# Tokens dealt to partitions four in a row: 4 KB runs of DRAM per partition in place of four 1 KB runs

## The chip, the cores and the metric

The kernel runs on one core of one Trainium2 chip. The metric is the device time of one execution in microseconds (us); each kernel was run several times. Ratios are the mean time of one kernel's fast runs over the mean time of the other's fast runs of the same rounds, with a 95% interval, so they are not quite the ratio of the medians that stand beside them.

Names: TensorE (PE in the profile) multiplies matrices, VectorE (DVE) and ScalarE (ACT) work elementwise, SyncE (SP) issues DMAs. A "tile" is 128 tokens, one on each partition; a "chunk" is four tiles, 512 tokens.

## The reference, cut to what matters

```python
x = A_x                                   # 2048 tokens x 512, bf16
x = x + A(layernorm(x), wqkv, wo)         # linear attention, 32 heads of 16
x = x + B(layernorm(x), w1, w2)           # 512 -> 1376, relu, -> 512
x = x + A(layernorm(x), wqkv, wo)
x = x + B(layernorm(x), w1, w2)

# inside A: every token's k and v are summed over all tokens, no mask
kv  = einsum("bhsd,bhse->bhde", phi(k), v)
z   = einsum("bhsd->bhd", phi(k))
o   = (phi(q) @ kv) / (phi(q) . z)
```

Everything but `kv` and `z` is done token by token, and those two are sums over all tokens. So it doesn't matter which token sits on which partition, as long as the output is written back through the same assignment.

## The kernel before

The program builds a list of 1316 operations, and two tables then fix the order of the instructions on every engine (`ORDER`) and the PSUM bank, the buffer that a matmul writes to, of every result (`BANKS`). Each engine gets its instructions in that order.

```python
# token n*128 + p sits in tile n on partition p
x_v   = A_x[0].rearrange("(n p) d -> p n d", p=128)
out_v = out[0].rearrange("(n p) d -> p n d", p=128)
def ld_x(t, lo=0):                                       # one chunk, 512 KB
    dma(lambda e, t=t: e.dma_start(xin[:, 4*t+lo:4*t+4, :], x_v[:, 4*t+lo:4*t+4, :]), ...)
dma(lambda e: e.dma_start(xin[:, 0, :], x_v[:, 0, :]), ...)   # tile 0 alone, 128 KB
ld_x(0, 1)                                               # tiles 1 to 3, 384 KB
dma(... wqkv[:, :, D:2*D] ...)                           # key weights, 512 KB
for t in range(1, NCH):
    ld_x(t)
    if t == 1: dma(... wqkv[:, :, 0:D] ...)              # query weights
# [cut: value weights, wo; w1 and w2 much later]

# TensorE starts with ten dummy matmuls; nothing else is ready yet
for k in range(WARM): last = e.matmul(psv[:, wt, :], wrm[:, 0:128], wrm[:, :], ...)

# chunk 0: per tile, statistics (VectorE), 1/std (ScalarE), norm (VectorE),
# transposes (TensorE), copy to Tb (ScalarE or VectorE), key projection (TensorE)

def store_chunk(t):          # chunks 0 to 2: one DMA; the last chunk: tile by tile
    for (lo, hi) in segs:
        dma(lambda e, lo=lo, hi=hi: e.dma_start(out_v[:, lo:hi, :], xn[:, lo:hi, :]), ...)
# [cut: everything between]
```

Of the kernel before, what the change touches and what calls it, by code (L numbers as in the profile page):

```python
# [69 lines left out]
class _Graph:  # L70
# [46 lines left out]
    def add_flex(self, alts, reads=(), writes=(), name=""):  # L117
# [7 lines left out]
17 0 14 12 15 18 13 1 16 19 2 20 22 3 24 4 21 23 25 5 6 26 27 7 28 8 47 29 33 30 31 32a 48 34 40 49 35 71 50 36 41 42  # L125
51 37 43 52 72 44 38 73 53d 45 56 87 46a 58 39a 81 89 54 88 60 76 83 59 57 55 61 82 93 62 74 63 78 75 115 98 77 94 79
117 103 95 64 80 65a 108 113 66a 119 86 68a 120 118 116 69 114 92 121 84 67a 122 85 90 135 99 91 70 105 123 141 125d
100 124d 154 104 128 230 109 126d 130 127d 110 156 129 136 132 155 160 131 142 133 138 134 137 158 148 143 101 96 147
150 161 157 159 162 97 144 163 171 139 149 140 145 189 172 146 102 164 177 190 166d 165d 168a 167d 153 169 151 178 152
176 106 191 111 170 107 173 192 183 222 179 112 174 182 9 180 184 193 10 185 223 175 195 11 181 186 188 187 196 219  # L130
220 197 221 213 198 199 207 215 214 201 216 208 217 209 194 203 210 202 200 211 204 205 206 231 212 232 233 218 234
224 261 228 262 225 229 263 226 239 235a 236d 237a 238d 244 240 264 241 259 265 246 242 245 243 266 254 268 260 249
256 270 255 313 269 317 314a 276 267 251 257 315 318a 311 252 271 316a 312d 250 258 339 247 273 248 272 253 334 340
278 277 319 335 329 320 341 336 342d 338 344 330 337a 331 286 332d 333 345 349 321 296 346 288 347d 281 298 322 350
297 323 291 343 299 289 274 287 324 275 306 292 327 293 290 301 307 279 280 308 358 328 303 326 302 370 325 359a 362
371a 309 227 282 388 283 363d 348 398 389 284 392 393 285 399 378 304 403 379 305 394 402 360 404 397 376 294 380 300
405 351 407 310 374 381 361a 382 368 377a 295 375a 390 400 395 383 352 369a 410 437 386 355 438 411 385 396a 364 356d
439 384 372 357 365a 387 406a 366 440 373a 441 457 367a 353 412 354 401a 442 458 447 391a 473 413 409 452 448 462 408
453 451 443 456 480 444 477 461 474 478 493 475 494 445 496 449 450d 417 446 419 476 418a 463 427 420a 454 466 455d
414 479 467 428a 423 459 464 415a 465d 460a 469 425 470 416 471 481 472 424a 495 421 426d 468 497 435 422a 429 572  # L140
436a 433 430a 431 434a 482 432a 484 483 498 488 499 485 489 504 486 500 505 487 501 521 502 503 490 526 491 522 492
506 547 507 525 536 508 509 510 527 531 548a 511 530 512 570 550 513 549 532 552 551a 514 571 515a 554 516d 518a 556
573 519 517a 537 558 553a 520 555a 538 533 560 534d 557a 539d 559a 566 523 528 542 524d 561a 529d 562 567a 543 541 535
564 563d 540 574 565a 544 545 575 546 577 576 568 578 579 569a 581 580 714 590 591 715 582 592 593 583 595 594 584 585
596 597 586 716 618 717 587 598 620 619 588 601 621 629 589 622 602 623 631 599 630 643 632 600 633 625 635 624 626
603 648 645 604 644 606 653 605 607 627 646 650 628 663 608 649 636 664d 655 609 647 654 665 610 670 651 638 652 656
637 666 634 671d 668 667a 611 612a 613d 672 669d 614a 616 674 673d 615a 639 676 675d 617 640 718 677a 657 641 719 678
720 680 679a 723 681a 682 724 721 683a 729 722 684 730 725 685a 734 792 735 793 737 726 736 738 739 794 741 740 731
742 727 745 732 728 796 746 733 743 797 658 798 744 795 801 660 747 659 799 802 748 807 800 812 749 750 751 808 686
752 753 661 754 813 662 687 803 688 814 755 817 756a 757d 809 693 818 758a 810 760 823 695 689 690 815 811 696 691 804  # L150
816 694 759a 642 805 824 806 819 761 697 820 698 825 692 821 826 822 699 827 828 829 700 830 831 706 832 702 701 707
703 833 834d 835a 713 704 709 836d 838 762 708 705 837a 768 764 710 839 769 711 763 765 712 775 771 770 776 766 772
767 783 777 778 782 785 773 779 784 774 873 840 874 780 875 786 781 791 842 841 846 787 843 852 788 848 847 858 854
849 844 853 845 789 860 855 859 851 850 790 857 863 861 856 862 866 876 867 877 864 868 895 865 896 878 897 872d 870a
869d 883 871a 898 879 899 893 880 885 881 900 894 884 888 903 905 890 904 889 902 949 951 950a 925 901 952a 891 945
907 892 947 910 946a 948d 906 908 968 886 911 882 909 912 963 887 927 969 926 973 964 972 913 953 974 967 978 965 954
970 975 966d 930 971d 976a 979 983 955 915 980 932 981d 920 956 917 984 957 916 935 922 914 918 921 958 919 936 940
923 924 937 959 931 1012 962 998 1013 960 942 989 961 1014 992 990a 943 1015 941 991 1006 1016 999a 993d 982 996 933
1007a 928 934 994 997a 929 944 977 1032 938 995a 939 985 1037 1033 1034 1027 1038 1035a 1039 1022 1028 1040a 1029 1008
1031 1023 1043 1030a 1024 1000 1025d 1026 986 1042 987 1004 988 1001d 1041 1044 1109 1010 1005a 1009a 1071 1011a 1017  # L160
1002 1018 1036 1019 1072 1057 1021 1003a 1048 1073 1020 1058a 1051 1107 1049a 1074 1111 1052a 1050 1075 1112 1108 1076
1081 1110 1053 1078 1077 1086 1054a 1079 1055 1080 1087 1059 1056a 1045 1090 1046 1061 1082 1047 1060a 1083 1063 1084d
1062a 1088 1113 1085 1067 1089a 1065 1064a 1101 1068a 1069 1066a 1091 1070a 1096 1092 1093 1095 1114 1097 1125 1094d
1100 1189 1116 1126 1115 1128 1098 1117 1099a 1127 1118 1190 1102 1121 1129 1130 1122 1119 1131 1191 1123 1135 1132
1136 1120 1133 1124 1177 1134 1137 1145 1178a 1138 1192 1139 1140 1146 1150 1141 1149 1155 1151 1144 1147 1166 1142
1156 1148a 1169 1152 1167a 1157 1143d 1154 1153d 1160 1175 1158d 1170a 1103 1104 1159 1171 1105 1162 1106 1161 1176a
1173 1172d 1163 1168 1181 1164 1174a 1165 1179 1182a 1193 1180a 1183 1194 1184a 1185 1195 1196 1186a 1198 1197 1187
1199 1200 1188a 1210 1245 1201 1211 1207 1246 1208 1247 1203 1214 1204 1209 1215 1202 1229 1205 1212 1230a 1206 1225
1213 1216 1222 1226a 1248 1227 1223a 1224 1217 1228a 1233 1218 1219 1231 1234a 1220 1221 1235 1232a 1237 1236a 1239
1238a 1249 1240a 1250 1252 1251 1241 1253 1254 1242a 1243 1255 1259 1244a 1263 1260 1278 1261 1264 1262 1256 1265 1266  # L170
1279 1268 1282 1269 1267 1273 1280 1257 1274 1270 1258 1299 1281 1283 1300 1296 1284 1297 1287 1298 1275 1271 1288
1276 1301 1272 1285 1302 1292 1277 1286 1303 1293 1307 1304 1305 1289 1308 1306 1309 1294 1290 1295 1315 1310 1291
1314 1311 1313 1312
"""
BANKS = ("0145346702076132532532355225315253131235215113532321551212533251266701701076152313542613074562174032"
         "6357657130422400110424124141114204120144220014202421014221040214120410204224101021404031605473414160"
         "275136027534461275403172566403241570613247")
# [46 lines left out]
def build_kernel(nc, A_x, A_wqkv, A_wo, B_w1, B_w2, out, n_layers_pairs=2, Q_LATE=3, O_PE_CHUNKS=3, PHI_PATH=3,  # L224
# [17 lines left out]
    with es:  # L242
# [110 lines left out]

        x_v = A_x[0].rearrange("(n p) d -> p n d", p=128)
        out_v = out[0].rearrange("(n p) d -> p n d", p=128)
        def ld_x(t, lo=0):
            dma(lambda e, t=t: e.dma_start(xin[:, 4 * t + lo:4 * t + 4, :], x_v[:, 4 * t + lo:4 * t + 4, :]),
                [], [("xin", i) for i in range(4 * t + lo, 4 * t + 4)], (1150.0, 2400.0, 1500.0, 1500.0)[t], "ld_x%d" % t)
        dma(lambda e: e.dma_start(xin[:, 0, :], x_v[:, 0, :]), [], [("xin", 0)], 50.0, "ld_x0a")  # L359
        wq_v = A_wqkv.rearrange("(c p) n -> p c n", p=128)  # L360
        ld_x(0, 1)
        dma(lambda e: e.dma_start(wqkv[:, :, D:2 * D], wq_v[:, :, D:2 * D]), [], [("wk",)], 1650.0, "ld_wk", eng=ACT if WK_ACT else SP)
        for t in range(1, NCH):
            ld_x(t)
            if t == 1:
# [445 lines left out]
        def store_chunk(t):  # L811
# [3 lines left out]
            for (lo, hi) in segs:  # L815
                dma(lambda e, lo=lo, hi=hi: e.dma_start(out_v[:, lo:hi, :], xn[:, lo:hi, :]),
                    [("xn", i) for i in range(lo, hi)] + [("T", i) for i in range(NT)], [("out", t, lo)],
                    400.0 * (hi - lo), "st%d_%d" % (t, lo))
# [265 lines left out]
```

## Time and profile before

280.0 us, median of 3 runs (279.91 to 280.34). These lines are from the page of before: busy time of the engines, the chain of work that ended last by engine, and the DMA queue (packets, MB, share of 16 engines' time).

```profile
span 278.0 us, 4780 instructions
PE 273.4 (98%) x1804; PEld 154.2 (55%) x1804; DVE 221.0 (80%) x567; ACT 176.6 (64%) x367; POOL 34.5 (12%) x43
...
q1 hardware_dynamic: 44368, 17.96, 27.8%
...
q14 instruction: 8, 0.07, 0.1%
...
PE 96%; DVE 1%; DMA 1%; ACT 0%; issue 0%; SPq 0%; DVEq 0%
```

TensorE is busy 98% of the span and makes up 96% of the chain; DMA is 1% of it. "Busy" hides small waits: matmuls overlap in the trace (one of 512 columns is listed with 379 ns, and the next can start 216 ns after it). The distances between their starts show the waits. They are 216 ns for 512 columns, 109 ns for 256 and 43 ns for 96. Summed for all 1804 matmuls at those rates this is 267.8 us, and the real distances are only 5.8 us longer.

Where the 1% of DMA lies is seen in the chain in order of time (start, us, what):

```profile
1.25 3.18 DMA xin<-in_A_x_dram
4.43 0.02 issue
4.46 0.69 DVE bst L418
5.15 0.33 DVE xn L845
5.47 0.05 issue
5.52 0.41 PE ps L474 x4
```

The chain waits for tiles 1 to 3 (issued at 1.25 us, landed at 4.43), goes through VectorE and reaches TensorE at 5.5 us. From 6.6 us on it stays on TensorE until 272.8 us. The same stretch in the timeline (start, us, engine, line, operation, in brackets the idle time before and what ended it):

```profile
3.07 0.69 DVE L418 BATCH_NORM_STATS2 bst<-xin 128x6 f32<-128x512 bf16 x1 [1.89 <-DMA xin<-in_A_x_dram]
4.46 0.69 DVE L418 BATCH_NORM_STATS2 bst<-xin 128x6 f32<-128x512 bf16 x1 [0.47 <-DMA xin<-in_A_x_dram]
5.07 0.40 DVE L845 TENSOR_SCALAR xn<-xin,mv,rstd 128x512 bf16<-128x512 bf16 x1
5.52 0.40 PE L474 MATMUL ps<-ident,xn 128*128 128x128 bf16 x4
5.95 0.60 ACT L481 ACTIVATE Tb<-ps 128x512 bf16<-128x512 bf16 x1 [1.41 <-PE ps L474]
6.61 1.04 PE L511 MATMUL ps<-wqkv,Tb 128*128 128x512 bf16 x4 [0.26 <-ACT Tb L481]
```

VectorE waits twice for x (for tile 0, then for tiles 1 to 3), tile 0's norm stands behind the statistics of a later tile, and the first projection (6.61 us) comes 2.17 us after tiles 1 to 3 landed. The part on DMA issues gives the size and the time from issue to landing of each load:

```profile
xin<-in_A_x_dram SPq DMA_DIRECT2D x3, 512.0 KB, 8.1
out_dram<-xn SPq DMA_DIRECT2D x3, 512.0 KB, 2.9
...
xin<-in_A_x_dram SPq DMA_DIRECT2D x1, 384.0 KB, 3.2
...
xin<-in_A_x_dram SPq DMA_DIRECT2D x1, 128.0 KB, 2.3
```

### The profile page before, as it was taken

What the parts mean: (1) busy time and instruction counts of PE and PEld (TensorE: products, weight loads), DVE (VectorE), ACT (ScalarE), POOL (GpSimd) and SP (SyncE); (2) the same over time, 40 slices, a digit from 0 to 9 for tenths busy, and PEclk for the clock granted to TensorE, in tenths of its full rate; (3) what the DMA queues carried; (4) which work ended last, traced back from release to release, by engine and by line L of the source; (5) the groups of instructions that cost most, each with busy time, mean ns of one, the idle gap of its engine ahead of it and who ended that gap; (6) DMA issues with size and microseconds to landing.
All of it is one profiled execution on the core that took longest, in us unless ns stands there. A gap on an engine that the chain in (4) does not pass through costs nothing.

```text
span 278.0 us, 4780 instructions
## 1 busy us (share of the span) xinstructions
PE 273.4 (98%) x1804; PEld 154.2 (55%) x1804; DVE 221.0 (80%) x567; ACT 176.6 (64%) x367; POOL 34.5 (12%) x43
## 2 busy tenths in 40 slices
PE   7999999999999999999999999999999999999995
PEld 2444454444475747755777444544454675675784
DVE  5999759999995796986798786799989497282686
ACT  3998728998856494496157874899894617415100
POOL 3111000000301021042003473000011002000000
PEclk9999999999999999999999999999999999999999
DMA  6976940120314036014004210004131115103004
GB/s 215 348 165 67 297 150 0 24 54 0 59 38 94 2 64 107 2 19 76 2 0 58 57 38 2 0 1 79 22 72 21 38 38 143 29 2 96 0 2 151
DMA packets 44534, 18.32 MB, mean 66 GB/s; under 512 B 36352, under 2 KB 44000, under 8 KB 44512
## 3 DMA queue, kind: packets, MB, share of 16 engines
q1 hardware_dynamic: 44368, 17.96, 27.8%
q8 instruction: 14, 0.23, 0.4%
q10 hardware_dynamic: 144, 0.07, 0.1%
q14 instruction: 8, 0.07, 0.1%
HBM read 7.01 MB, written 2.10 MB: 33 GB/s over the span
## 4 chain that ended last, share of the span: by engine, by line
PE 96%; DVE 1%; DMA 1%; ACT 0%; issue 0%; SPq 0%; DVEq 0%
PE ps L511 95%; DMA xin<-in_A_x_dram 1%; DVE xn L551 1%; PE ps L474 0%; DVE bst L418 0%; ACT Tb L481 0%; DVE xn L805 0%; SPq L359 0%; DVEq L1022 0%; DVE xn L845 0%
## 5 line engine op out<-in xcount | busy, mean ns | idle before, releaser
L511 PE MATMUL ps<-Tb,w 128*128 128x512 bf16 x320 | 73.9, 379 | 0.0
L710 ACT ACTIVATE big<-ps 128x512 bf16<-128x512 f32 x70 | 40.5, 597 | 37.9 <-PE ps L511 37.8
L511 PEld LDWEIGHTS ps<-Tb,w 128*128 128x128 bf16 x320 | 30.8, 98 | 33.2 <-DMA Tb<-xn 0.2
L771 DVE SCALAR_TENSOR_TENSOR xres<-ps,rstdf,xres 128x256 f32<-128x256 f32 x64 | 29.9, 480 | 21.8 <-PE ps L511 21.0
L518 ACT ACTIVATE sqscr<-xres 128x512 bf16<-128x512 f32 x48 | 30.2, 631 | 19.4 <-DVE xres L555 14.9
L493 ACT ACTIVATE escr<-ps 128x512 bf16<-128x512 f32 x64 | 37.8, 614 | 6.2 <-PE ps L511 6.1
L491 ACT ACTIVATE big<-ps 128x512 bf16<-128x512 f32 x64 | 38.4, 617 | 3.8 <-PE ps L511 3.8
L511 PE MATMUL ps<-w,big 128*128 128x256 bf16 (+1 forms) x224 | 34.3, 273 | 0.0
L511 PE MATMUL ps<-wqkv,Tb 128*128 128x512 bf16 x128 | 30.9, 379 | 0.4 <-ACT Tb L481 0.3
L511 PE MATMUL ps<-big,xn 128*128 128x512 bf16 x128 | 31.1, 379 | 0.0
L497 DVE TENSOR_TENSOR big<-big,emscr 128x512 bf16<-128x512 bf16 x64 | 29.3, 469 | 2.2 <-ACT big L491 0.8
L511 PE MATMUL ps<-Tb,wqkv 128*128 128x512 bf16 x128 | 30.4, 379 | 0.0
L511 PE MATMUL ps<-Wp,big 128*128 128x512 bf16 x128 | 30.2, 379 | 0.0
L544 POOL TENSOR_TENSOR rstdf<-varf,nhalf 128x4 f32<-128x4 f32 x8 | 8.9, 1115 | 128.3 <-DVE varf L542 109.2
L511 PEld LDWEIGHTS ps<-w,big 128*128 128x128 bf16 (+1 forms) x224 | 21.7, 98 | 4.9 <-DVE xres L771 0.6
L495 DVE TENSOR_SCALAR emscr<-escr 128x512 bf16<-128x512 bf16 x64 | 19.9, 320 | 4.8 <-ACT escr L493 4.7
L511 PE MATMUL ps<-w2s,xin 128*128 128x256 bf16 x160 | 22.1, 273 | 0.0
L511 PE MATMUL ps<-w,xin 128*128 128x256 bf16 x160 | 22.1, 272 | 0.0
L669 DVE TENSOR_TENSOR big<-big,ps 128x512 bf16<-128x512 bf16 x32 | 20.3, 680 | 1.0 <-PE ps L511 0.8
L511 PEld LDWEIGHTS ps<-Tb,wqkv 128*128 128x128 bf16 x128 | 12.2, 98 | 14.5 <-issue 0.7
L511 PEld LDWEIGHTS ps<-wqkv,Tb 128*128 128x128 bf16 x128 | 12.0, 98 | 14.8 <-ACT Tb L481 1.0
L511 PEld LDWEIGHTS ps<-Wp,big 128*128 128x128 bf16 x128 | 11.9, 98 | 14.9 <-ACT Wp L600 1.0
(103 smaller groups left out, 330.3 us busy)
## 6 DMA issues: line engine op xcount, KB each, us to landing
wqkv<-in_A_wqkv_dram SPq DMA_DIRECT2D x3, 512.0 KB, 7.2
xin<-in_A_x_dram SPq DMA_DIRECT2D x3, 512.0 KB, 8.1
out_dram<-xn SPq DMA_DIRECT2D x3, 512.0 KB, 2.9
w<-in_B_w_dram SPq DMA_DIRECT2D x1, 1376.0 KB, 6.6
w<-in_B_w_dram SPq DMA_DIRECT2D x1, 1280.0 KB, 9.7
wo<-in_A_wo_dram SPq DMA_DIRECT2D x1, 512.0 KB, 9.0
Tb<-xn SPq DMA_TRANSPOSE x30, 3.2
xin<-in_A_x_dram SPq DMA_DIRECT2D x1, 384.0 KB, 3.2
```

What stands on the lines that cost most here:

```text
L491: g.add(ACT, lambda e: e.activation(dst_ap, psv[:, b, :], ACTF.Identity, bias=1.0 + 1e-6, scale=1.0), [("ps", b)], [dst_key], C_ACT_PSUM, ...
L493: g.add(ACT, lambda e: e.activation(escr[:, s, :], psv[:, b, :], ACTF.Exp), [("ps", b)], [("escr", s)], C_ACT_EXP, name=name + "_exp")
L495: g.add(DVE, lambda e: e.tensor_scalar(emscr[:, s, :], escr[:, s, :], 1.0, 1e-6, ALU.min, ALU.add), [("escr", s)], [("emscr", s)], C_DVE_B ...
L497: g.add(DVE, lambda e: e.tensor_tensor(dst_ap, dst_ap, emscr[:, s, :], ALU.max), [dst_key, ("emscr", s)], [dst_key], 340.0, name=name + "_ ...
L511: last = e.matmul(o, l, r, start=st, stop=sp, skip_group_check=skip)
L518: g.add(ACT, lambda e: e.activation(sqscr[:, q, :], xres[:, i, :], ACTF.Square, accum_out=dst[:, i:i + 1]), [("xres", i)], [("sqscr", q), ...
L544: g.add(POOL, lambda e: e.tensor_tensor(rstdf[:, sl], varf[:, sl], nhalf[:, 0:4], ALU.pow), [("varf", t), ("nhalf",)], [("rstdf", t)], C_P ...
L551: g.add(DVE, lambda e: e.scalar_tensor_tensor(xn[:, i, :], psv[:, b, :], rstdf[:, i:i + 1], xres[:, i, :], ALU.mult, ALU.add), rd, [("xn", ...
L669: g.add(DVE, lambda e, j=j: e.tensor_tensor(unit_ap(us[j]), unit_ap(us[j]), psv[:, GB[j], :], ALU.mult), [("big", us[j]), ("ps", GB[j])], ...
L710: g.add_flex([(ACT, lambda e, M=M, b=b, u=u: e.activation(unit_ap(u, M), psv[0:M, b, :], ACTF.Relu), C_ACT_PSUM), (DVE, lambda e, M=M, b=b ...
L771: g.add(DVE, lambda e: e.scalar_tensor_tensor(xres[:, i, cols], psv[:, bank, R], rstdf[:, i:i + 1], xres[:, i, cols], ALU.mult, ALU.add), ...
```

## The change

Tokens are dealt to partitions four in a row: within a chunk, partition p holds tokens 4p to 4p+3, one in each of the four tiles. A partition's part of a chunk is then one run of 4 KB in DRAM, for the loads of x and the chunk stores of the output. The intent is cheaper DMA. Instruction order and PSUM banks were searched anew for it.

```diff
-x_v = A_x[0].rearrange("(n p) d -> p n d", p=128)
-out_v = out[0].rearrange("(n p) d -> p n d", p=128)
+x_v = A_x[0].rearrange("(t p i) d -> p t i d", p=128, i=4)
+out_v = out[0].rearrange("(t p i) d -> p t i d", p=128, i=4)
 def ld_x(t, lo=0):
-    ... x_v[:, 4*t+lo:4*t+4, :] ... (1150.0, 2400.0, 1500.0, 1500.0)[t]
+    ... x_v[:, t, lo:4, :]      ... (1150.0, 2800.0, 1400.0, 1400.0)[t]   # estimates for the search
-dma(... xin[:, 0, :], x_v[:, 0, :] ...)
+dma(... xin[:, 0, :], x_v[:, 0, 0, :] ...)
-    out_v[:, i, cols]                    # half-tile stores at the end
+    out_v[:, i // 4, i % 4, cols]
-    out_v[:, lo:hi, :]                   # chunk and tile stores
+    out_v[:, t, lo - 4*t:hi - 4*t, :]
-ORDER = """ ... 1316 entries ... """     BANKS = ( ... )
+ORDER = """ ... 1316 entries, other order ... """     BANKS = ( ... other banks ... )
```

## The prediction

> **What bounds the kernel now.** TensorE. The page gives PE 273.4 of 278.0 us (98%), DVE 80%, ACT 64%. The chain of waits is 96% PE, unbroken from 6.6 to 272.8 us but for pieces of 0.01 to 0.07 us; only its head (DMA of x 3.18 us, statistics, first norm) and tail (last residuals, store) are anything else. Busy time hides small stalls, so I took the start-to-start distances of the 1804 matmuls from the trace: 216 ns for 512 columns, 109 for 256, 43 for 96, with almost no spread. At those rates the matmuls need 267.8 us. The distances exceed that by 5.8 us: 1.9 us in the cold warm-up, 0.7 us before the first projection, 0.4 us at 22.9 and 24.0 us, the rest some thirty stalls of 0.08 to 0.2 us, most at changes of matmul kind, which come with any order. Even a perfect schedule has only 2 to 3 us to win, 1%.
>
> **What the change does.** (1) Chunk loads of x and three output stores get 4 KB runs (3 KB for the first chunk's remainder) instead of 1 KB. In the trace's DMA packet records a 1,024-byte packet takes 46 ns, a 2,752-byte one 109, a 512-byte one 27: about 8.5 ns fixed. The Trainium skill ("DMA: Bandwidth & Descriptors", section "Why small descriptors are slow (HBM only)") also names a fixed overhead per packet, about 3 cycles. Estimate from the fit: 158 ns for 4 KB against 184 for four 1 KB packets, 14%. Per engine that is 0.14 us off the first 384 KB, 0.21 us off each 512 KB load; the last x chunk would land 0.5 to 0.8 us earlier. (2) Tile 0 is read as 1 KB pieces 4 KB apart, the half-tile stores at a larger pitch: same packets, about equal. (3) Arithmetic is unchanged: tokens are permuted alike in input and output, and attention sums over all. (4) Instruction order and PSUM banks are all new; this, not the DMA, touches the 267 us in the middle.
>
> **How much is critical.** The x DMAs are critical only until 5.2 us. DVE waited 0.5 us for tiles 1 to 3 (landing at 4.43) with tile 0's norm queued behind; but the warm-up ends only at 5.46 and the first transpose starts at 5.52, so earlier landing wins under 0.1 us there, perhaps 0.1 more at 7.5. Chunk 1 landed at 8.24, when VectorE was just coming free; between 7 and 20 us VectorE and ScalarE are full, so earlier chunks 1 to 3 win nothing. The large stores overlap PE. The last piece is still a half tile (left instead of right, on SyncE instead of ScalarE): 2.9 us after the last matmul, as before.
> Sum: head -0.1 us; stalls redistributed, 0 plus or minus 0.8; tail 0 plus or minus 0.1.
>
> **Predicted: 279.8 us**, 8 times in 10 between 278.8 and 281.0. Faster by over 2%: 2%; within 2%: 95%; slower by over 2%: 3%.
>
> **What would show it.** DMA packets: 1,920 1 KB packets of x and 1,536 of the output replaced by about a quarter as many, near 158 ns each. First real projection still at 6.5 to 6.6 us. Chain still 96% PE. Nominal sum unchanged at 267.8 us; excess 5 to 6.5 us, in other places.
>
> **What would make it wrong.** If rows are not merged, packets stay at 1 KB and the DMA doesn't change. If 4 KB runs land later (the change itself raises its model's latency for chunk 1), chunk 1's norms slip and PE idles around 18 to 24 us. If the new order puts VectorE evictions late, small PE waits add up.

## The result, and the profile after

The changed kernel took 279.98 us (median of 4 runs, 279.74 to 280.14), before 280.07 us in the same rounds: ratio 0.9995, interval 0.9978 to 1.0012. The time is the same. The lines of its page that answer to those of before:

```profile
span 277.9 us, 4796 instructions
PE 273.7 (98%) x1804; PEld 154.4 (56%) x1804; DVE 221.3 (80%) x568; ACT 176.3 (63%) x366; POOL 33.3 (12%) x43
...
q1 hardware_dynamic: 41808, 17.96, 27.6%
...
PE 96%; ACT 1%; DVE 1%; DVEq 0%; issue 0%
```

The data queue has 2,560 packets less: 3,456 of 1 KB are gone, and there are 768 of 4 KB and 128 of 3 KB. In the trace's packet records a 4 KB packet takes 159 ns (median), a 3 KB one 121 ns and a 1 KB one 46 ns. The DMA is indeed better once it runs. These windows (from : to, length, busy us of each engine with its instructions, granted clock, DMA share, GB/s) show before first, then after:

```profile
2.00:5.00 3.00, 3.00 (x8) 1.06 (x7) 1.42 (x3) 0.57 (x3) 1.35 (x3) 1.00 0.93 306
8.00:12.00 4.00, 4.00 (x25) 1.87 (x23) 3.93 (x14) 4.00 (x10) 0.62 (x1) 1.00 1.06 359
```

```profile
2.00:5.00 3.00, 3.00 (x8) 1.06 (x7) 1.51 (x4) 0.57 (x3) 1.35 (x3) 1.00 0.95 306
8.00:12.00 4.00, 4.00 (x27) 1.86 (x25) 4.00 (x14) 4.00 (x9) 0.00 (x0) 1.00 1.05 402
```

From 8 to 12 us the DMA moved 402 GB/s in place of 359. The nine traces with 4 KB runs show 395 to 403 GB/s there, and those of before, e2, e5 and e6 with 1 KB runs 350 to 359. From 2 to 5 us, while tiles 1 to 3 are on their way, for which the chain waits, it moved 306 GB/s in both. Between 8 and 12 us VectorE and ScalarE are full (4.00 and 4.00 of 4 us), so faster landing finds nobody waiting. The start of after's timeline:

```profile
3.20 0.69 DVE L418 BATCH_NORM_STATS2 bst<-xin 128x6 f32<-128x512 bf16 x1 [2.02 <-DMA xin<-in_A_x_dram]
4.36 0.69 DVE L418 BATCH_NORM_STATS2 bst<-xin 128x6 f32<-128x512 bf16 x1 [0.25 <-DMA xin<-in_A_x_dram]
4.97 0.40 DVE L845 TENSOR_SCALAR xn<-xin,mv,rstd 128x512 bf16<-128x512 bf16 x1
5.48 0.63 PE L474 MATMUL ps<-ident,xn 128*128 128x128 bf16 x4
6.15 0.60 ACT L481 ACTIVATE Tb<-ps 128x512 bf16<-128x512 bf16 x1 [1.47 <-PE ps L474]
6.80 1.14 PE L511 MATMUL ps<-wqkv,Tb 128*128 128x512 bf16 x4
```

Tiles 1 to 3 landed 0.10 us earlier here (4.34 us against 4.44), and tile 0's norm began 0.10 us earlier. Yet the first projection starts 0.19 us later. The four transposes took 0.63 us in place of 0.40: they stand 106 ns apart, as against 55 ns in before. The trace's clock records say why. TensorE went from half to full rate at 7.05 us in this execution, at 5.10 us in before's.

The sum of matmul distances above nominal is 5.79 us after, 5.78 before. The waits are in other places: those between 20 and 75 us fell from 1.40 to 0.57 us, those between 170 and 200 us rose from 0.65 to 1.08 us, and the head rose from 2.85 to 3.13 us.

This table, made from the records of all traces, is used below. "Lands" is the last of the 16 semaphore increments of a load; "clock full" the time at which TensorE's clock record goes to full rate; "first" and "second" are the starts of the first and second group of key projections; "stretch" runs from the second group to the start of the last matmul; "tail" from there to the end of the span. All in us; they can differ by 0.01 from the views. Runs e1 to e12 are described in the next section.

| run | order | tile 0 lands | tiles 1-3 land | key weights land | chunk 1 lands | chunk 3 lands | clock full | first | second | stretch | tail |
|---|---|---|---|---|---|---|---|---|---|---|---|
| before | old | 3.05 | 4.44 | 6.00 | 8.27 | 12.98 | 5.10 | 6.61 | 8.49 | 266.35 | 3.14 |
| after | new | 3.18 | 4.34 | 6.42 | 8.37 | 12.37 | 7.05 | 6.80 | 8.69 | 266.16 | 3.08 |
| e1 | old | 3.28 | 4.49 | 6.55 | 8.48 | 12.51 | 4.98 | 6.68 | 8.55 | 266.60 | 3.24 |
| e2 | new | 2.94 | 4.40 | 6.34 | 8.66 | 13.18 | 5.48 | 6.57 | 8.46 | 266.34 | 3.05 |
| e3 | new | 3.29 | 4.53 | 6.44 | 8.64 | 12.66 | 3.98 | 6.70 | 8.59 | 266.10 | 3.08 |
| e4 | old | 3.00 | 4.58 | 6.52 | 8.58 | 14.90 | 7.03 | 6.97 | 8.85 | 266.41 | 4.23 |
| e5 | old | 2.95 | 5.02 | 8.20 | 9.72 | 14.24 | 5.68 | 8.34 | 10.10 | 266.88 | 3.42 |
| e6 | old | 2.90 | 4.38 | 6.47 | 7.96 | 12.49 | 4.88 | 6.60 | 8.44 | 266.14 | 4.01 |
| e7 | new | 2.92 | 4.52 | 6.25 | 8.41 | 12.40 | 5.91 | 6.82 | 8.71 | 266.14 | 3.08 |
| e8 | new | 2.92 | 4.81 | 6.88 | 8.56 | 12.56 | no record | 7.01 | 8.87 | 266.48 | 3.34 |
| e9 | new | 2.87 | 3.67 to 4.36 | 7.78 | 9.10 | 13.16 | 5.40 | 7.91 | 9.68 | 266.16 | 3.45 |
| e10 | new | 2.88 | 3.27 to 4.41 | 6.84 | 8.16 | 12.21 | 4.91 | 6.98 | 8.74 | 266.14 | 3.45 |
| e11 | new | 3.23 | 5.05 | 6.59 | 8.13 | 12.38 | no record | 7.22 | 9.11 | 266.11 | 3.06 |
| e12 | old | 3.24 | 4.42 | 6.45 | 8.55 | 12.56 | 4.46 | 6.59 | 8.48 | 266.59 | 3.24 |

The traces of e5, e6, e7, e8 and e12 lack 17 or 18 of the 1804 matmul records; starts and landings don't suffer from that, sums of distances would, so none is quoted from them.

### The profile page after: what moved, and what is told of

The parts are those of the page before. It is cut to its first block, busy times and chain, and to the rows that moved or that the text cites. A ratio compares the mean times of both kernels' runs of the same rounds, so it can differ in the third digit from the quotient of the medians.

```text
span 277.9 us, 4796 instructions
## 1 busy us (share of the span) xinstructions
PE 273.7 (98%) x1804; PEld 154.4 (56%) x1804; DVE 221.3 (80%) x568; ACT 176.3 (63%) x366; POOL 33.3 (12%) x43
## 3 DMA queue, kind: packets, MB, share of 16 engines
HBM read 7.01 MB, written 2.10 MB: 33 GB/s over the span
## 4 chain that ended last, share of the span: by engine, by line
PE 96%; ACT 1%; DVE 1%; DVEq 0%; issue 0%
PE ps L511 94%; PE ps L395 2%; DVE xn L551 1%; PE ps L474 0%; ACT sqscr L518 0%; DVE xres L524 0%; ACT lden L658 0%; ACT xn L529 0%; ACT lden L660 0%; ACT escr L493 0%; ACT big L491 0%; DVEq L1022 0%; DVE xn L805 0%; DVE wrm L388 0%
## 5 line engine op out<-in xcount | busy, mean ns | idle before, releaser
L710 ACT ACTIVATE big<-ps 128x512 bf16<-128x512 f32 x70 | 41.3, 596 | 26.6 <-PE ps L511 26.4
L491 ACT ACTIVATE big<-ps 128x512 bf16<-128x512 f32 x64 | 38.5, 623 | 2.2 <-PE ps L511 2.1
L495 DVE TENSOR_SCALAR emscr<-escr 128x512 bf16<-128x512 bf16 x64 | 21.2, 338 | 5.2 <-ACT escr L493 4.9
L544 POOL TENSOR_TENSOR rstdf<-varf,nhalf 128x4 f32<-128x4 f32 x8 | 8.0, 1008 | 127.5 <-DVE varf L542 68.7
L511 PEld LDWEIGHTS ps<-Wp,big 128*128 128x128 bf16 x128 | 12.0, 98 | 14.6 <-issue 0.7
```

The lines of the kernel that those rows point to most:

```text
L491: g.add(ACT, lambda e: e.activation(dst_ap, psv[:, b, :], ACTF.Identity, bias=1.0 + 1e-6, scale=1.0), [("ps", b)], [dst_key], C_ACT_PSUM, ...
L495: g.add(DVE, lambda e: e.tensor_scalar(emscr[:, s, :], escr[:, s, :], 1.0, 1e-6, ALU.min, ALU.add), [("escr", s)], [("emscr", s)], C_DVE_B ...
L511: last = e.matmul(o, l, r, start=st, stop=sp, skip_group_check=skip)
L544: g.add(POOL, lambda e: e.tensor_tensor(rstdf[:, sl], varf[:, sl], nhalf[:, 0:4], ALU.pow), [("varf", t), ("nhalf",)], [("rstdf", t)], C_P ...
L710: g.add_flex([(ACT, lambda e, M=M, b=b, u=u: e.activation(unit_ap(u, M), psv[0:M, b, :], ACTF.Relu), C_ACT_PSUM), (DVE, lambda e, M=M, b=b ...
```

## The experiments

Theory T: TensorE is at its floor, the large loads have slack, and the head varies with the time at which TensorE's clock rises. Rival G: the layout wins something and the new order gives it back. Rival S: tile 0, now read in pieces 4 KB apart, lands later and delays the head. All kernels gave correct results.

| run | what | median us | before, same rounds | ratio | 95% interval |
|---|---|---|---|---|---|
| e1 | layout only | 280.47 | 280.36 | 1.0000 | 0.9985 to 1.0015 |
| e12 | layout only, again | 280.47 | 280.19 | 1.0009 | 0.9996 to 1.0023 |
| e2 | order only | 280.04 | 280.36 | 0.9984 | 0.9969 to 0.9999 |
| e3 | after, again | 279.92 | 280.36 | 0.9987 | 0.9968 to 1.0005 |
| e11 | after, third time | 280.28 | 280.35 | 0.9991 | 0.9973 to 1.0009 |
| e4 | x chunks 1-3 in 256-byte runs | 281.69 | 280.36 | 1.0047 | 1.0026 to 1.0068 |
| e5 | x tiles 1-3 in 256-byte runs | 281.35 | 280.44 | 1.0033 | 1.0011 to 1.0054 |
| e6 | x chunks 1-3 tile by tile | 280.98 | 280.44 | 1.0016 | 0.9999 to 1.0033 |
| e7 | after, chunk 0 not dealt | 279.92 | 280.44 | 0.9983 | 0.9968 to 0.9998 |
| e8 | after, tile 0 contiguous | 279.97 | 280.44 | 0.9981 | 0.9966 to 0.9996 |
| e9 | e7, tiles 1-3 by three DMAs | 280.76 | 280.35 | 1.0008 | 0.9985 to 1.0031 |
| e10 | e9 with nine warm-up matmuls | 280.70 | 280.35 | 1.0007 | 0.9989 to 1.0025 |

### e1 and e12: the layout alone, in the old order

```diff
 # before, with x_v and out_v (and their uses) as in the change; ORDER and BANKS stay
```

> The 4 KB runs with the instruction order and banks of before. Theory T (TensorE at its floor, loads hidden): 279.8 to 280.2 us, ratio to before within 0.999 to 1.001; the packets of x and of the output are 4 KB; first projection between 6.5 and 6.6 us if the TensorE clock goes to full rate before 5.5 us in this execution, near 6.8 us if it does so after 6.5 us. Rival G (the runs win 0.3 to 0.5 us and the new order gives it back): 279.5 to 279.7 us. Rival S (tile 0's pieces 4 KB apart land 0.13 us later and that delays the head): first projection near 6.8 us whatever the clock does.

> The 4 KB runs in the old order once more. In its first trace the stretch from the second group of projections to the last matmul took 266.60 us, 0.25 more than before's and 0.45 more than after's, and VectorE started chunk 1's statistics when chunk 1 landed (8.48, 8.50 us) instead of having it ready. Theory O (the old order has no slack for chunk 1, the new one has): if chunk 1 lands 0.2 us or more before the second group of projections starts, that stretch takes 266.3 to 266.4 us; if it lands 0.1 us before it or later, 266.5 to 266.7 us; time 280.1 to 280.6 us, ratio to before 0.999 to 1.001. Rival (the layout itself slows the middle): 266.6 us whatever the landing. Packets of 4 KB, last x chunk lands near 12.5 us in either case.

Measured: ratios 1.0000 and 1.0009. The layout alone wins nothing, so rival G falls. (e1 took 280.47 us, above theory T's 279.8 to 280.2, and its first projection started at 6.68 us with an early clock, where 6.5 to 6.6 was expected.) Tile 0 landed at 3.28 and 3.24 us, chunk 3 at 12.51 and 12.56 us. The stretch took 266.60 and 266.59 us, 0.25 more than in before. In both traces chunk 1 landed late (8.48 and 8.55 us) and VectorE, whose next instruction in the old order is that chunk's statistics, took it at once. VectorE and TensorE lines of the timeline of before, then of e1:

```profile
8.35 2.46 DVE L418 BATCH_NORM_STATS2 bst<-xin 128x6 f32<-128x512 bf16 x4
14.54 3.62 PE L511 MATMUL ps<-big,xn 128*128 128x512 bf16 x16
```

```profile
8.50 2.47 DVE L418 BATCH_NORM_STATS2 bst<-xin 128x6 f32<-128x512 bf16 x4
14.60 3.74 PE L511 MATMUL ps<-big,xn 128*128 128x512 bf16 x16
```

VectorE begins 0.15 us later (8.50 against 8.35) and is full from there on, and the sixteen matmuls at 14.6 us now contain a wait of 0.12 us, which before's don't, and the waits near 23 and 24 us grow too (0.43 us in before, 0.59 in e1). e12's expectation was met, but since chunk 1 again landed late it doesn't exclude that the layout itself slows the middle.

The waits near 23 and 24 us have a nearer cause: there TensorE waits for DMA transposes of normed tiles (Tb<-xn), as this line of e1's timeline says:

```profile
23.27 2.10 PE L511 MATMUL ps<-wqkv,Tb 128*128 128x512 bf16 x8 [0.22 <-DMA Tb<-xn]
```

The third transpose landed at 22.81 us in before and TensorE went on at 22.95; in e1 it was 23.14 and 23.27. Of these 0.33 us only 0.09 come from a later issue (17.92 against 17.83 us); the rest is a longer transfer (5.2 us in place of 5.0), and whether the layout causes that wasn't tested. The same landing goes with the other stretches of the old order: 22.58 us in e6 (stretch 266.14), 24.98 in e5 (266.88). So e6 isn't evidence for chunk 1's landing: that came 0.31 us earlier than in before, but VectorE took it only 0.06 us earlier. The late chunk 1 is thus shown to cost about 0.12 us of the 0.25; the rest stays open.

### e2, e3 and e11: the order alone, and the changed kernel again

```diff
 # e2: before, with ORDER and BANKS of after; e3 and e11: after, unchanged
```

> The 1 KB runs with the instruction order and banks of after. Theory T: 279.8 to 280.2 us, matmul distances beyond nominal 5 to 6.5 us. Rival G: 280.3 to 280.5 us, the order being the loss. Rival S: tile 0 contiguous again, so first projection near 6.6 us whatever the clock does.

> The changed kernel once more, for a tighter ratio and a second look at when TensorE's clock rises (5.10 us in the trace of before, 7.05 us in that of after). Theory T: 279.8 to 280.1 us; the rise falls somewhere else between 4.6 and 8.1 us, and the first projection follows it (6.5 to 6.6 when early, 6.8 when late). Rival C (the rise is a property of the kernel): again near 7.05 us.

> The changed kernel a third time, on the same chip as the two above, as their yardstick and for one more look at the clock: 279.8 to 280.1 us; tile 0 lands at 3.15 to 3.3 us; first projection 2.17 us after tiles 1 to 3 land if the clock rose by 5.5 us, up to 2.46 us if near 7 us; from the second group of projections to the last matmul 266.1 to 266.2 us.

Measured: 0.9984, 0.9987 and 0.9991. The order alone does what the whole change does. If anything it is a small gain, not the loss that rival G needed, and a bit more than theory T expected: the interval of e2 just excludes 1. All runs with the new order and a plain load of chunks (after, e2, e3, e7, e8, e11) have ratios from 0.9981 to 0.9995; the two with the new layout and the old order have 1.0000 and 1.0009.

As to the clock, the rise came at 3.98 us in e3, where after had 7.05 (4.6 to 8.1 was expected): it isn't a property of the kernel. From the landing of tiles 1 to 3 to the first projection it took 2.17 to 2.22 us in before, e1, e2, e3, e6 and e12 (rise by 5.5 us), 2.30 us in e7 (rise at 5.91) and 2.46 and 2.39 us in after and e4 (rise at 7.05 and 7.03). The late rise thus cost after about 0.25 us at the head. The Trainium skill ("TensorE: Matmul & The Clock Gate", section "Part 1: The HAM clock gate (the "warmup" mystery)") says that TensorE runs at half rate until it has been active for a window of about 3.4 us that runs freely, not from the kernel's start. These traces agree in kind: the first matmul starts at 1.24 us in all, and the rise came 2.7 to 5.8 us later, a spread of 3.1 us. (2.7 us is less than one such window of activity.)

e11 missed part of its expectation: tiles 1 to 3 landed at 5.05 us, the first projection started 2.17 us after that, and its median was 0.36 us above e3's. The first of the 16 increments of that load came at 3.71 us, the fifteenth at 4.36, the last at 5.05; TensorE had to wait for this last one. (That the engines of one DMA finish independently and the semaphore counts them is stated in the Trainium skill, "DMA: Bandwidth & Descriptors", section "Why a DMA increments its semaphore by 16 and not by 1"; here the spread is 1.34 us.)

### e4 and e6: the opposite of the change for chunks 1 to 3, and its control

```diff
 # e4, from before: each load of chunks 1-3 cut into four DMAs by columns, 256-byte runs
-    dma(lambda e, t=t: e.dma_start(xin[:, 4*t+lo:4*t+4, :], x_v[:, 4*t+lo:4*t+4, :]), ...)
+    n = 4 if t > 0 else 1
+    cols = [slice(q*512//n, (q+1)*512//n) for q in range(n)]
+    dma([lambda e, t=t, c=c: e.dma_start(xin[:, 4*t+lo:4*t+4, c], x_v[:, 4*t+lo:4*t+4, c]) for c in cols], ...)
+ # a list shares one semaphore; its users wait for 16 times its length
 # e6: the same four DMAs, cut by tiles: xin[:, r, :] <- x_v[:, r, :], 1 KB runs
```

> The opposite of the change, larger: before, with x chunks 1 to 3 loaded in 256-byte runs (each load cut into four DMAs by columns). By the packets (18 ns for 256 bytes against 46 ns for 1 KB, estimate) each of the three loads takes 0.8 us longer, chunk 1 lands near 9.1 us instead of 8.3, chunk 3 near 15.5 instead of 13.0. Theory T (these loads have slack because VectorE and ScalarE are full until 20 us): 279.9 to 280.5 us, at most 0.5 us of new TensorE idling between 18 and 28 us. Rival L (chunk loads gate the start): 281 us or more.

> Control for the run with 256-byte runs: before, with x chunks 1 to 3 each loaded by four DMAs of one tile, still in 1 KB runs: as many DMA instructions as that run, packets as in before. There the last matmul was only 0.4 us later than in before, but the end came 4.2 us after it instead of 3.2, with one 8 KB instruction fetch of 833 ns on the DMA engines just when the last store ran. Theory F (nine more instructions move that fetch in front of the end): again 281.2 to 281.7 us, last matmul 274.7 to 275.2, and the end 4.0 us or more after it, with an 8 KB fetch near 277 us. Rival L (the late x chunks cost the time): 280 to 280.5 us, the end 3.2 us after the last matmul.

By its time, e4 seemed to prove the rival: 281.69 us, 1.3 us slower than before. The trace puts most of it elsewhere. Chunk 3 landed at 14.90 us, 1.9 us later than in before, and the stretch is 266.41 us, only 0.06 more. (Chunk 2, at 12.55 us in place of 11.47, did make VectorE wait 0.27 us, and TensorE fell back by a further 0.35 us at 17 us; but 0.30 of that was made up at the waits near 23 and 24 us, which shrank. Chunk 1 landed at 8.58 us, earlier than the 9.1 expected, so e4 hardly tests it.) The head is 0.36 us later, with a late clock (7.03 us) and tiles 1 to 3 at 4.58 us. What remains, 1.09 us, is in the tail: 4.23 us against 3.14. The half tile that is stored last is 128 packets, eight for each of 16 DMA engines. 120 of them started between 277.0 and 277.4 us, the other eight only at 278.0 us and after. One 8 KB packet of the "instruction" kind had started at 277.17 us and took 833 ns, until 278.00. The packet records don't name the engine, but eight packets are one engine's share and they start when that fetch ends; the last increment of the store's semaphore came at 278.78 us, the first at 277.58.

The control e6 has the DMA instructions of e4 and the packets of before. It expected the same loss. By the medians it lost 0.54 us (280.98 against 280.44, 0.2 us below the stated range), where e4 lost 1.33. Its trace shows the same collision: tail 4.01 us, first increment of the last store at 276.88 us and last at 277.89, an instruction packet of 599 ns at 276.50 us, and eight of the 128 packets behind it. Its last matmul came even earlier than before's (274.57 against 274.84). The page counts the fetch; the lines of the DMA queues in e4, then in e6:

```profile
DMA packets 49287, 18.33 MB, mean 66 GB/s; under 512 B 42640, under 2 KB 48752, under 8 KB 49264
...
q14 instruction: 9, 0.07, 0.1%
```

```profile
DMA packets 44679, 18.33 MB, mean 66 GB/s; under 512 B 36496, under 2 KB 44144, under 8 KB 44656
...
q14 instruction: 9, 0.07, 0.1%
```

Before has 8 such packets within its span; the ninth comes at 279.6 us, after its end. Nine more DMA instructions moved it in front of the end, where it hit the last store. So in the traces the largest part of e4's loss, 1.09 of 1.51 us, is a side effect of how the experiment was made, and the control has it too (0.88 us). The control doesn't account for all of it: e4 is still 0.7 us slower than e6 by the medians. Between their two traces e4 is 0.41 us later at the second group (later landing of tiles 1 to 3, later clock), 0.27 us longer in the stretch and 0.22 us in the tail. So by these single traces the late chunks cost between 0.06 us (stretch against before) and 0.27 us (against e6); the timed runs leave no trace, so the rest of the 0.7 us stays open. Without the control the whole 1.3 us would have been put down to them.

### e5: the opposite of the change for tiles 1 to 3

```diff
 # from before, as e4, but
-    n = 4 if t > 0 else 1
+    n = 4 if t == 0 else 1
```

> Before, with only the first chunk's remaining 384 KB (tiles 1 to 3) in 256-byte runs, cut into four DMAs by columns. In the six traces so far the first projection starts 2.17 us after these tiles land (2.17 to 2.19 when TensorE's clock rose by 5.5 us), or 2.39 to 2.46 us when it rose near 7.0 us. Estimate from the packets: landing near 5.1 us instead of 4.44. Theory H (the head is this landing plus a fixed chain): first projection at 7.2 to 7.6 us, last matmul later by 0.4 to 0.8 us than in before's 274.84. Rival W (the warm-up or other loads hide it): first projection below 6.9 us. Theory F (an extra instruction fetch collides with the last store when there are more DMA instructions, see the next run) would add 1.1 us between last matmul and end.

Measured: 281.35 us, ratio 1.0033. Tiles 1 to 3 landed at 5.02 us, but the first projection started only at 8.34 us, beyond the expected range, because the key weights, queued behind them, landed at 8.20 us. These were also issued later, at 3.30 us in place of 1.71, behind three more DMA instructions, and e5 had no control; so it isn't shown how much of this is due to the 256-byte runs. The head does depend on the first megabyte of loads: with the key weights 2.2 us later than in before, the second group of projections starts 1.6 us later and the last matmul 2.1 us later in this execution, though it was the slowest of the four (282.22 us; the others 280.77 to 281.44). The tail (3.42 us) shows no collision; the instruction packet came at 281.2 us, after the end.

### e7 and e8: tile 0 contiguous again

```diff
 # e7, from after: chunk 0 as in before
+x_0   = A_x[0].rearrange("(t i p) d -> p t i d", p=128, i=4)
+out_0 = out[0].rearrange("(t i p) d -> p t i d", p=128, i=4)
-    x_v[:, t, lo:4, :]
+    (x_v if t else x_0)[:, t, lo:4, :]          # tile 0 and the store of chunk 0 likewise
 # e8, from after: tile 0 = tokens 0 to 127, tiles 1-3 dealt from tokens 128 to 511
+x_0   = A_x[0][128:512].rearrange("(p i) d -> p i d", i=3)
```

> After, but chunk 0 dealt as in before (tile 0 one contiguous 128 KB piece, tiles 1 to 3 in 1 KB runs, its output store too); chunks 1 to 3 keep 4 KB runs; no instruction more or less. Tile 0 landed at 3.18 to 3.29 us in the three traces with pieces 4 KB apart, at 2.94 to 3.05 in the three without. Theory S2 (the pitch costs tile 0 0.2 us): tile 0 lands at 2.9 to 3.05 us; tiles 1 to 3 at 4.4 to 4.55; first projection 2.17 us after that with an early clock; time 279.7 to 280.0 us. Rival N (chance): tile 0 lands at 3.2 us again.

> After, with tile 0 the first 128 tokens (contiguous) and tiles 1 to 3 dealt from tokens 128 to 511 in contiguous 3 KB runs; chunk 0's store is two DMAs (one instruction more). Theory H with S2: tile 0 at 3.0 us, tiles 1 to 3 at 4.3 us or a little earlier (packets save 0.14 us, estimate), first projection near 6.45 us with an early clock, time 279.5 to 279.8 us. Rival N: tiles 1 to 3 at 4.45 to 4.55 us and nothing gained. Theory F: if the one instruction more is enough, the end comes 4 us after the last matmul and the time is near 280.8 us.

Tile 0 landed at 2.92 us in both. Over all traces the two groups don't overlap: 2.87 to 3.05 us where tile 0 is one contiguous piece (9 traces), 3.18 to 3.29 us where its 1 KB pieces are 4 KB apart (5 traces). Rival S is right about the landing. But it costs nothing that can be measured: VectorE then waits for tiles 1 to 3 anyway, e3 with tile 0 at 3.29 us began its first projection 2.17 us after those, and e7 and e8 take as long as e3 (279.92 and 279.97 against 279.92).

The hope of e8, tiles 1 to 3 landing earlier from one contiguous piece with 3 KB runs, failed: 4.81 us. In the six traces with 3 KB runs they landed at 4.34 to 5.05 us, in the five with 1 KB runs and one DMA behind an unchanged start (before, e2, e4, e6, e7) at 4.38 to 4.58 us. The packet records of after show what eats the saving: of the 128 packets of 3 KB, among the first of the kernel, 23 took more than one and a half times the median of 121 ns, up to 478 ns; of the 384 packets of 4 KB that load later chunks it was 16. A saving of 0.14 us per DMA engine is smaller than the spread of these first packets. Why they are slow wasn't tested. One part of e8 stays open: its stretch is 0.3 us longer than that of the other runs with the new order, mostly in front of matmuls near 47 us.

### e9 and e10: tiles 1 to 3 one by one, and a shorter warm-up

```diff
 # e9, from e7: tile 3 first, then 2, 1, each with its own semaphore, in VectorE's order
-    xin[:, 1:4, :] <- one DMA
+    xin[:, 3, :] ; xin[:, 2, :] ; xin[:, 1, :] <- three DMAs
 # e10, from e9
-    WARM=10
+    WARM=9
```

> The kernel of the run with chunk 0 plain, with tiles 1 to 3 loaded by three DMAs, each with its own semaphore, tile 3 first, in the order in which VectorE takes them (two DMA instructions more). Theory H (the head is a chain on VectorE that starts when these tiles land; it sat idle 0.2 to 0.5 us before them): tile 3 lands near 3.5 us instead of 4.5, VectorE takes it at once at 3.9 us, tile 0's norm is done near 5.0 us. Theory W (the warm-up then holds): the tenth warm-up matmul ends at 5.5 us in any case with a late clock, so the first transpose starts at 5.45 to 5.5 us, first projection 6.5 to 6.6 us, the second group of projections near 8.4 us instead of 8.7, time 279.6 to 279.9 us. Without W, the first transpose would start near 5.05 us.

> The same with nine warm-up matmuls in place of ten. H and W together: first transpose near 5.1 us, first projection at 6.1 to 6.5 us (the key weights, landing at 6.2 to 6.9 us in the traces so far, may become what it waits for), second group near 8.1 to 8.4 us, last matmul 274.2 to 274.6 us, time 279.3 to 279.7 us: 0.3 us below the changed kernel. Rival (the clock rises later with less warm-up, or something else gates the head): no better than 279.9 us.

VectorE's idle time before tiles 1 to 3 did vanish: tile 0's norm started at 4.40 us in place of 4.97. The timeline of e9 shows both things that then stood in the way, and e10 the second alone:

```profile
4.40 0.41 DVE L848 TENSOR_SCALAR xn<-xin,mv,rstd 128x512 bf16<-128x512 bf16 x1
5.44 0.39 PE L477 MATMUL ps<-ident,xn 128*128 128x128 bf16 x4
...
7.91 1.02 PE L514 MATMUL ps<-wqkv,Tb 128*128 128x512 bf16 x4 [1.65 <-DMA wqkv<-in_A_wqkv_dram]
```

```profile
4.41 0.41 DVE L848 TENSOR_SCALAR xn<-xin,mv,rstd 128x512 bf16<-128x512 bf16 x1
4.98 0.39 PE L477 MATMUL ps<-ident,xn 128*128 128x128 bf16 x4
...
6.97 1.02 PE L514 MATMUL ps<-wqkv,Tb 128*128 128x512 bf16 x4 [1.17 <-DMA wqkv<-in_A_wqkv_dram]
```

In e9 the norm ends at 4.81 us and the first transpose starts at 5.44, when the warm-up matmuls are through; with one warm-up matmul less it starts at 4.98 us. So the warm-up hides what an earlier landing wins, as the prediction said. Then the key weights are the next gate: TensorE waited 1.65 and 1.17 us for them. They were issued at 2.64 us in place of 1.71, behind two more DMA instructions, and landed at 7.78 and 6.84 us. Neither kernel is faster than before (1.0008, 1.0007). The expected 279.3 to 279.9 us was missed, in part for a reason that the expectation of e10 names. The other part is in the tail: 3.45 us in both, 0.37 more than in after, though the last store landed 2.49 us after the last matmul's start as in after. e5 and e8, which also have one to three DMA instructions more, have long tails too (3.42 and 3.34 us); why wasn't tested.

No experiment beat the changed kernel. Order only, e7 and e8 are equal to it within the noise.

## Why the prediction was right or wrong

**The time** was right: 279.8 us predicted, 279.98 measured, within 278.8 to 281.0, and "within 2%" at 95%. TensorE at 98% busy and 96% of the chain, the unchanged nominal sum (267.8 us) and the excess (5.79 us, predicted 5 to 6.5, in other places) were read rightly. That the number came within 0.2 us is partly luck: in the profiled execution the first projection started 0.19 us later than in before instead of 0.1 earlier, and the stretch was 0.19 us shorter, so the two cancel.

**The DMA once it runs** was right: 3,456 packets of 1 KB replaced, 159 ns for 4 KB (158 predicted from a fit to the trace before), chunk 3 landing 0.61 us earlier (0.5 to 0.8 predicted). The Trainium skill's fixed overhead per packet ("DMA: Bandwidth & Descriptors", section "Why small descriptors are slow (HBM only)") agrees in kind: 46 ns for 1 KB and 159 ns for 4 KB leave some 8 ns per packet (46 minus a third of the difference of 113).

**"Per engine that is 0.14 us off the first 384 KB"** was not borne out. The load came 0.10 us earlier in the one trace of after, but over the traces 3 KB runs landed no earlier than 1 KB runs, with a wider spread. The fit was made of packets in full stream, and these are the first packets.

**"Tile 0 is read as 1 KB pieces 4 KB apart: same packets, about equal"** was wrong: same packets, but 0.13 to 0.42 us later. It was harmless, since tiles 1 to 3 gate the head.

**"Head -0.1 us"** and the first projection "at 6.5 to 6.6 us" were wrong: 6.80 us. In after's trace this is the late rise of TensorE's clock, worth about 0.25 us by the distances from landing to first projection; with early clocks it was 6.68, 6.70 and 6.59 us in e1, e3 and e12. The prediction didn't see that the warm-up ends in a state that differs from execution to execution.

**"Chunk 1 landed when VectorE was just coming free, so earlier chunks win nothing"** was right: chunks 2 and 3 landed earlier in e1 and e12 (chunk 3 at 12.51 and 12.56 us) and won nothing. The slack of the later chunks is limited, as e4 shows: with chunk 2 landing 1.08 us and chunk 3 1.9 us later the stretch grew by 0.06 us (against before) to 0.27 us (against e6). The prediction missed the other side. In the old order chunk 1 had only 0.08 us to spare (landed 8.27, used 8.35), so with the landings of the new layout the old order is the slower one (stretch 266.6 us, about 0.12 of the 0.25 us more by this). The new order puts another VectorE instruction first and takes chunk 1 at 8.82 us when it landed at 8.37. What it gains in the stretch, 0.19 us against before and 0.44 us against e1, is of the size of the small gain that the ratios of the new order show. The clearest change in the traces is another one: before's 0.43 us of waiting for the third and fourth DMA transposes near 23 and 24 us is gone. In after the third landed at 23.28 us and TensorE began its next matmuls on transposed tiles only at 23.83, with other work in between. How much each place contributes wasn't isolated; the waits moved in many places.

So the layout gains nothing, because it speeds up loads that had slack and doesn't speed up the one that hadn't. The new order is at best a little better by itself; the traces suggest, but don't show, that this is because it loosens places that the old one had left tight.

Open: some runs of before took 281.0 to 281.5 us with no such run among those of after, e2, e3, e7, e8 and e11 (at most 280.72); timed runs leave no trace, so the cause wasn't seen. They widen the intervals and push the ratios of the new order down a little: by the medians of the same rounds it gains 0.02 to 0.19%.

## What to carry to other kernels

Before making a transfer cheaper, look who waits when it lands: here 12% more bandwidth came in a stretch where the consumers were full, and none in the 3 us in which TensorE depended on loads of x. A load at the very start is judged by its slowest DMA engine and by what is queued behind it, so moving small pieces to the front can just hand the wait to the next load. And when an experiment adds instructions, give it a control that adds them without the suspected cause, and read where in the trace the time went before believing its total.

## What the Trainium skill lacked or had wrong

- "TensorE: Matmul & The Clock Gate", Part 1, gives the rise of the clock as around 4 us into sustained activity, plus or minus 500 ns. Here it came 2.7 to 5.8 us after the first matmul (at 3.98 to 7.05 us, first matmul at 1.24 us, twelve traces). The spread of 3.1 us fits its own remark about a free-running window of 3.4 us better than plus or minus 500 ns; the 2.7 us doesn't fit a full window of activity.
- "DMA: Bandwidth & Descriptors" names a fixed overhead of about 3 cycles per packet but not that early packets of a kernel can be slower: of the 128 packets of 3 KB, 13 to 23 took over 1.5 times the median of 121 ns in the six traces that have them (in after's 23, up to 478 ns), and these loads landed no earlier than with 1 KB packets.
- The same page doesn't say that the pitch of equal runs in DRAM matters at a few KB: a 128 KB load in 1 KB runs landed at 2.87 to 3.05 us when contiguous and at 3.18 to 3.29 us with the runs 4 KB apart.
- No page gives a figure for what an instruction fetch can cost a data transfer that runs at the same time (it would belong to "Runtime: NRT & Kernel Launch"): one 8 KB fetch, of 599 ns in e6 and 833 ns in e4, held up eight packets of the last store, which landed 0.8 and 1.0 us later than in before, and nine more DMA instructions were enough to move it there.
